# Attention and a gated feed-forward in one kernel: the transposes of q and k move from the matrix engine to DMA

## The chip, the core and the metric

The kernel runs on one core of one Trainium2 chip. The time is device microseconds from the start to the end of one execution, as the median of several runs, and lower is better. The engines of the core run beside each other and wait for each other by semaphores: PE (TensorE, matrix products, with PEld loading the stationary operand), DVE (VectorE), ACT (ScalarE), POOL (GpSimd), and SP (SyncE), which here only issues DMAs. Every instruction of an engine runs in the order in which the program holds it.

## The reference

```python
def _attn_ref(q, k, v):                       # q, k, v: (8, 12, 448, 64) float32
    S = q.shape[2]
    scale = 1.0 / np.sqrt(q.shape[-1])
    scores = scale * np.matmul(q, k.transpose(0, 1, 3, 2)) - np.log(S)
    attn = 1.0 / (1.0 + np.exp(-scores))
    return np.matmul(attn, v)

def _moe_ref(x, w_in, w_out):                 # x: (3584, 768), w_in: (768, 2048)
    h = x @ w_in
    g = h - np.tanh(h)
    return g @ w_out
```

The attention's output, with its heads side by side, is x: 8 batches of 448 tokens, 768 features each. w_in and w_out are given as float64.

## The kernel before, in words

**Two halves of every number.** A product in float32 takes PE longer than one in float16, so most products are made from float16 parts. A number times a power of two is rounded to float16 (the high part), and what is left over is rounded to float16 again (the low part). A product is then three float16 products: high by high, high by low, low by high. Each pair of parts takes two instructions: a scaled copy on ACT or DVE, and one `scalar_tensor_tensor` on DVE for the remainder.

**Batches.** Eight batches go through the kernel. For a batch there is attention (six pairs of heads), then `moe1` (x times w_in, lines 668 to 692, and the gate's function in `mix`), then `moe2` (g times w_out, line 798 and, for the last 64 tokens, line 836). Batch 0's attention is made alone at the start, in float32 (`attention32`), while w_in and w_out are read and turned from float64 to float32. From then on the attention of batch b + 1 is put into `moe2` of batch b: a generator, `stream` (line 429), holds it in steps, and `second` takes the next step after each so many rows of `moe2`, by the tables `BLOCKS`, `BLOCKS0` and `BLOCKS1`. `BLOCKS` has twelve steps, four rows of `moe2` apart, which is two steps for each of a batch's six pairs of heads. In `moe1` of the batches from 1 on there is no step of the attention. What `stream` does ahead of its main loop (the first two pairs' parts among it) runs in batch 0's `moe1`.

**A pair of heads.** The pair is called g. q and k of a pair are loaded by `load_qk` with tokens on 112 partitions and 4 x 2 x 64 numbers on each (`kn`, `qn`). `norms` (line 308) squares and sums them on ACT, `scales` (line 316) adds the sums over the partitions with a product by ones and finds the power of two. Scores need the head's 64 numbers on partitions, so q and k are turned:

- `transpose` (line 299): four products with the identity on PE, in float32, into one tile of PSUM under the tag `tr`, of which there is one. `turn_k` also puts the sums of `scales` into the same tile's last columns.
- `parts` (lines 337 to 340): the high part from PSUM, on ACT (line 337) for all of Q and for some of K, on DVE (line 339) for the rest of K, then the low part from PSUM on DVE (line 340). They are written to K or Q (128 x 2 x 448, two buffers each), which `scores` (line 362) reads.

In `stream`'s main loop (line 508) step 0 of pair g turns q of pair g + 1, and step 1 turns k of pair g + 2. In both, the order on PE is: the turn, twelve products of scores for two blocks of 112 keys, then twelve products of the attention weights with v (line 386) for the blocks of the step before, then `moe2` again. ACT takes the sigmoid of the first block (line 371), then makes the high part of Q, then the second block's sigmoid, then the weights' high part (line 377); DVE makes the low parts. The loads of pair g + 3 are written in step 0, its norms in step 1. For the next batch's x, `batch_scales` (lines 608 to 631) finds one scale and splits x into parts on DVE (lines 625 and 626) at the end of each `moe2`.

PE, ACT, DVE and POOL run in the order in which the program is written. SP's order is the scheduler's.

**Weights.** `wi` and `wo` hold float32 blocks and, later, their float16 parts in the same memory: the float32 of block n lies `SHIFT` = 4 blocks further on, so the parts of block n overwrite float32 that has been used already.

Of the kernel before, what the change touches and what calls it, by code (L numbers as in the profile page):

```python
# [34 lines left out]
class Builder:  # L35
# [14 lines left out]
    SHIFT = 4  # L50

    def __init__(self, ctx, tc, q, k, v, w_in, w_out, out):
# [30 lines left out]
        self.wo = self.wp.tile([P, self.NF * 2 + self.SHIFT, 2, self.HALF], F16, name="wo")  # L83
# [29 lines left out]
    def where(self, kind, r, i=0):  # L113

        t, n, m = (self.wi, self.NB, 256) if kind == "in" else (self.wo, 1, self.HALF)
        f = t.rearrange("p a b c -> p (a b c)").bitcast(F32)
        r = r * n + i * self.NF + self.SHIFT
        return f[:, r * m : (r + n) * m]
# [91 lines left out]
    def split(self, t, n, S, act):  # L210

        F = t[:, n + self.SHIFT].rearrange("p b c -> p (b c)").bitcast(F32)
# [81 lines left out]
    def transpose(self, n, name, tag="tr", bufs=1, t=None):  # L294
        nc = self.nc
        if t is None:
            t = self.ps.tile([P, 512], F32, name=name, tag=tag, bufs=bufs)
# [13 lines left out]
    def scales(self, ss, pb):  # L311
# [3 lines left out]
        pb = pb[:, self.S : self.S + n]  # L315
# [16 lines left out]
    def parts(self, t, s, name, act):  # L332

        nc = self.nc
        o = self.qk.tile([P, 2, self.S], F16, name=name, tag=name)
        if act:
            nc.scalar.activation(o[:, 0], t, AF.Copy, scale=s)  # L337
        else:
            nc.vector.tensor_scalar(o[:, 0], t, s, None, op0=ALU.mult)
        nc.vector.scalar_tensor_tensor(o[:, 1], t, s, o[:, 0], op0=ALU.mult, op1=ALU.subtract)  # L340
        return o
# [87 lines left out]
    def stream(self):  # L429
# [559 lines left out]
```

## Time and profile before

| what | value |
|---|---|
| median of 3 runs | 1263.84 us (1262.47 to 1264.2) |
| the profiled execution: its own time | 1264.8 us |
| the profiled execution: span from first to last instruction | 1262.5 us |
| mean granted clock of PE | 0.995 |
| instructions | 20449 |
| DMA | 70.52 MB, mean 56 GB/s |

The profile is of one execution. A row of its groups gives the line, the engine, the operation, the tiles, the count, the busy time in us, the mean of one instruction in ns, and the idle time of the engine ahead of them with what ended it. PE's products overlap, so the duration of one is longer than the distance to the next; distances are read from the start times of the timeline. The span is 2.3 us shorter than the execution's own time.

### The profile page before, as it was taken

What the parts mean: (1) busy time and instruction counts of PE and PEld (TensorE: products, weight loads), DVE (VectorE), ACT (ScalarE), POOL (GpSimd) and SP (SyncE); (2) the same over time, 40 slices, a digit from 0 to 9 for tenths busy, and PEclk for the clock granted to TensorE, in tenths of its full rate; (3) what the DMA queues carried; (4) which work ended last, traced back from release to release, by engine and by line L of the source; (5) the groups of instructions that cost most, each with busy time, mean ns of one, the idle gap of its engine ahead of it and who ended that gap; (6) DMA issues with size and microseconds to landing.
All of it is one profiled execution on the core that took longest, in us unless ns stands there. A gap on an engine that the chain in (4) does not pass through costs nothing.

```text
span 1262.5 us, 20449 instructions
## 1 busy us (share of the span) xinstructions
PE 1235.0 (98%) x8011; PEld 685.3 (54%) x8011; DVE 946.7 (75%) x1473; ACT 940.2 (74%) x1325; POOL 38.6 (3%) x38
## 2 busy tenths in 40 slices
PE   9889889999999999999999999999999999999998
PEld 3245445555556555665555655555556655555555
DVE  5989988789876797676965798667976769645930
ACT  6957788958998688886878688886888868753820
POOL 0100000000010000100000000000000000000000
PEclk9999999999999999999999999999999999999999
DMA  9943254100122101220022200221012200100001
GB/s 261 299 126 90 56 162 136 49 20 1 36 73 57 42 2 42 65 65 7 1 58 64 56 1 16 64 58 41 1 43 67 62 7 1 28 14 20 1 13 32
DMA packets 114367, 70.52 MB, mean 56 GB/s; under 512 B 91872, under 2 KB 104416, under 8 KB 114272
## 3 DMA queue, kind: packets, MB, share of 16 engines
q1 hardware_dynamic: 113344, 69.00, 20.6%
q8 instruction: 63, 1.03, 0.3%
q10 hardware_dynamic: 928, 0.23, 0.1%
q14 instruction: 32, 0.26, 0.1%
HBM read 58.20 MB, written 11.01 MB: 55 GB/s over the span
## 4 chain that ended last, share of the span: by engine, by line
PE 74%; DVE 14%; ACT 6%; issue 3%; DMA 3%; SPq 0%; DVEq 0%; ACTq 0%
PE ph L676 30%; PE po L798 25%; PE sc L362 6%; PE acc L386 5%; PE por L836 3%; DVE ahl L378 2%; ACT a L371 2%; DVE xhl L626 2%; DMA raw<-moe_w_in 1%; PE acc L396 1%; PE qT L299 1%; DVE xhl L625 1%; ACT wo L214 1%; DVE stb L151 1%; DVE m L750 1%
## 5 line engine op out<-in xcount | busy, mean ns | idle before, releaser
L798 PE MATMUL po<-wo,g 128*128 128x384 f16 x2304 | 391.4, 326 | 1.0 <-ACT o L827 1.0
L676 PE MATMUL ph<-xhl,wi 128*128 128x448 f16 x2016 | 382.6, 352 | 0.0
L798 PEld LDWEIGHTS <-g 128*128 128x128 f16 x2304 | 219.5, 98 | 171.3 <-issue 30.4
L676 PEld LDWEIGHTS <-wi 128*128 128x128 f16 x2016 | 196.7, 98 | 185.0 <-issue 1.8
L371 ACT ACTIVATE a<-sc,nls,rn 112x896 f32<-112x896 f32 x168 | 179.9, 1095 | 45.4 <-PE sc L362 38.3
L378 DVE SCALAR_TENSOR_TENSOR ahl<-a,ahl 112x896 f16<-112x896 f32 x144 | 155.7, 1122 | 58.6 <-ACT ahl L377 57.9
L746 ACT ACTIVATE u<-ph,ih 128x896 f32<-128x896 f32 x64 | 64.4, 1006 | 98.9 <-PE ph L676 95.3
L377 ACT ACTIVATE ahl<-a 112x896 f16<-112x896 f32 x144 | 128.0, 939 | 0.0
L362 PE MATMUL sc<-Q,K 64*112 64x448 f16 x1008 | 116.1, 362 | 3.8 <-ACT a L371 2.8
L750 DVE SCALAR_TENSOR_TENSOR m<-ph,ihk,u 128x896 f32<-128x896 f32 x64 | 73.5, 1148 | 54.9 <-ACT th L748 54.6
L386 PE MATMUL acc<-ahl,vhl 112*64 112x448 f16 x864 | 96.4, 357 | 0.5
L660 ACT ACTIVATE g<-m,Sg 128x896 f16<-128x896 f32 x64 | 66.6, 1041 | 34.1 <-DVE m L764 28.7
L764 DVE COPY_PREDICATED m<-u,th 128x896 f32<-128x896 uint32 x64 | 77.3, 1207 | 6.9 <-DVE m L761 0.5
L661 DVE SCALAR_TENSOR_TENSOR g<-m,Sg,g 128x896 f16<-128x896 f32 x64 | 73.4, 1147 | 8.8 <-ACT g L660 8.8
L340 DVE SCALAR_TENSOR_TENSOR Q<-qT,sn,Q 128x448 f16<-128x448 f32 x42 | 28.6, 682 | 67.9 <-ACT Q L337 67.9
L362 PEld LDWEIGHTS <-K 64*112 64x112 f16 x1008 | 60.6, 128 | 32.5 <-issue 6.8
L761 DVE SCALAR_TENSOR_TENSOR m<-q,m 128x896 f32<-128x896 f32 x64 | 69.9, 1093 | 8.3 <-ACT q L760 0.9
L706 PE MATMUL ph<-x,wi 128*128 128x448 f32 x192 | 74.8, 539 | 0.0
L751 DVE SCALAR_TENSOR_TENSOR th<-ph,ih,th 128x896 f32<-128x896 f32 x64 | 73.3, 1145 | 0.0
L763 ACT ACTIVATE u<-u,b 128x896 f32<-128x896 f32 x64 | 66.7, 1043 | 5.6 <-DVE m L750 3.6
L757 DVE SCALAR_TENSOR_TENSOR m<-q,m 128x896 f32<-128x896 f32 x64 | 69.5, 1087 | 0.0
L386 PEld LDWEIGHTS <-vhl 112*64 112x64 f16 x864 | 43.5, 109 | 47.8 <-issue 26.1
(134 smaller groups left out, 1323.0 us busy)
## 6 DMA issues: line engine op xcount, KB each, us to landing
raw<-moe_w_in SPq DMA_DIRECT2D x24, 512.0 KB, 7.5
rawo<-moe_w_out SPq DMA_DIRECT2D x32, 384.0 KB, 3.9
kn<-k SPq DMA_DIRECT2D x96, 112.0 KB, 2.9
vn<-v SPq DMA_DIRECT2D x48, 224.0 KB, 2.7
qn<-q SPq DMA_DIRECT2D x94, 112.0 KB, 2.9
out<-o SPq DMA_DIRECT2D x7, 336.0 KB, 3.1
out<-o SPq DMA_DIRECT2D x7, 288.0 KB, 3.1
out<-o SPq DMA_DIRECT2D x7, 240.0 KB, 2.6
```

Source lines behind the costliest of these rows:

```text
L362: nc.tensor.matmul(ps[:CK, h, :S], K[r, w, cs], Q[r, x, :], start=(n == 0), stop=(n == len(prods) - 1))
L371: nc.scalar.activation(a, ps[:CK, :, :S], AF.Sigmoid, bias=self.nls[:CK], scale=scale)
L377: nc.scalar.activation(A[:, 0], a, AF.Copy, scale=A_SCALE)
L378: nc.vector.scalar_tensor_tensor(A[:, 1], a, A_SCALE, A[:, 0], op0=ALU.mult, op1=ALU.subtract)
L386: nc.tensor.matmul(acc[h * D : (h + 1) * D, : self.S], v[:, w, h, c, :], A[:, x, h], start=(c == 0 and n == 0), stop=(c == 3 and n == 2),)
L661: nc.vector.scalar_tensor_tensor(g[:, 1], m, Sg, g[:, 0], op0=ALU.mult, op1=ALU.subtract)
L676: nc.tensor.matmul(ph[:, e, :S], self.wi[:, c * self.NB + k, part, e * P : (e + 1) * P], xhl[c][:, x, :], start=(i == 0), stop=(i == 3 * s ...
L706: nc.tensor.matmul(ph[:, e, :S], self.where("in", c)[:, f * P : (f + 1) * P], xs[c], start=(c == 0), stop=(c == self.NC - 1),)
L750: V.scalar_tensor_tensor(m, ps, ihk, u, op0=ALU.mult, op1=ALU.mult)
L751: V.scalar_tensor_tensor(th, ps, ih, th, op0=ALU.mult, op1=ALU.subtract)
L764: V.copy_predicated(m, u.bitcast(U32), th)
L798: nc.tensor.matmul(po[i][:, :H], gs[f // 2][:, x, f % 2, tk * P : (tk + 1) * P], self.wo[:, i * self.NF + f, w], start=(f == 0 and n == 0) ...
```

## The change

The parts of q and k are made before the turn instead of after it, from `kn` and `qn` in SBUF with tokens on 112 partitions (512 numbers on each), into a float16 tile `w` (112 x 2 x 512), of which there is one. One DMA transpose, issued from SP, then writes both parts into K or Q: 8 blocks of 112 x 128. The turns on PE are gone, and the product of `scales` has a PSUM tile of its own under the same tag `tr`. To make room for `w`, the float32 of w_out lies three blocks ahead of its parts (`SHIFT_O` = 3); w_in keeps four.

```diff
     SHIFT = 4
+    SHIFT_O = 3
...
-        self.wo = self.wp.tile([P, self.NF * 2 + self.SHIFT, 2, self.HALF], F16, name="wo")
+        self.wo = self.wp.tile([P, self.NF * 2 + self.SHIFT_O, 2, self.HALF], F16, name="wo")
...
-        F = t[:, n + self.SHIFT].rearrange("p b c -> p (b c)").bitcast(F32)
+        F = t[:, n + (self.SHIFT if t is self.wi else self.SHIFT_O)].rearrange("p b c -> p (b c)").bitcast(F32)
...
-    def scales(self, ss, pb):
+    def scales(self, ss):
 
         nc = self.nc
         n = ss.shape[1]
-        pb = pb[:, self.S : self.S + n]
+        pb = self.ps.tile([P, 512], F32, name="pbn", tag="tr", bufs=1)[:, :n]
         nc.tensor.matmul(pb, self.onesf[:CK, :], ss, start=True, stop=True)
...
-    def parts(self, t, s, name, act):
-
-        nc = self.nc
+    def parts(self, n, s, name, act):
+
+        nc = self.nc
+        flat = n.rearrange("p c h d -> p (c h d)")
+        w = self.qk.tile([CK, 2, 4 * P], F16, name="w", tag="w", bufs=1)
+        if act:
+            nc.scalar.activation(w[:, 0], flat, AF.Copy, scale=s[:CK])
+        else:
+            nc.vector.tensor_scalar(w[:, 0], flat, s[:CK], None, op0=ALU.mult)
+        nc.vector.scalar_tensor_tensor(w[:, 1], flat, s[:CK], w[:, 0], op0=ALU.mult, op1=ALU.subtract)
         o = self.qk.tile([P, 2, self.S], F16, name=name, tag=name)
-        if act:
-            nc.scalar.activation(o[:, 0], t, AF.Copy, scale=s)
-        else:
-            nc.vector.tensor_scalar(o[:, 0], t, s, None, op0=ALU.mult)
-        nc.vector.scalar_tensor_tensor(o[:, 1], t, s, o[:, 0], op0=ALU.mult, op1=ALU.subtract)
+        nc.sync.dma_start_transpose(
+            o.rearrange("p x (c t) -> p (x c) t", c=4), w.rearrange("p x e -> p (x e)")
+        )
         return o
...
-        def turn(g, n, name):
-            return self.transpose(qk[g][n], name) if g < G else None
-
-        def turn_k(g):
-            if g >= G:
-                return None
-            t = self.ps.tile([P, 512], F32, name="kT", tag="tr", bufs=1)
-            turned = self.transpose(qk[g][0], "kT", t=t)
-            sc[g] = self.scales(ss.pop(g), t)
-            return turned
-
-        def parts_k(g, t):
+        def scales(g):
             if g < G:
-                K[g] = self.parts(t, sc[g][0][:, 0:1], "K", not splits(g) and g not in (2, 3))
-
-        def parts_q(g, t):
+                sc[g] = self.scales(ss.pop(g))
+
+        def parts_k(g):
             if g < G:
-                Q[g] = self.parts(t, sc[g][0][:, 1:2], "Q", True)
+                K[g] = self.parts(qk[g][0], sc[g][0][:, 0:1], "K", not splits(g) and g not in (2, 3))
+
+        def parts_q(g):
+            if g < G:
+                Q[g] = self.parts(qk[g][1], sc[g][0][:, 1:2], "Q", True)
                 qk.pop(g)
 
...
-            parts_k(g, turn_k(g))
+            scales(g)
+            parts_k(g)
             yield 450, False
-            parts_q(g, turn(g, 1, "qT"))
+            parts_q(g)
             load(g + 2)
...
-                    t = turn_k(g + 2)
-                elif g:
-                    t = turn(g + 1, 1, "qT")
+                    scales(g + 2)
                 pss = [self.scores(c, K[g], Q[g]) for c in (2 * i, 2 * i + 1)]
                 aa = [self.weigh(pss[0], sc[g][1][:CK, 0:1])]
                 if i:
-                    parts_k(g + 2, t)
+                    parts_k(g + 2)
                 elif g:
-                    parts_q(g + 1, t)
+                    parts_q(g + 1)
```

Where the instructions stand: first the PE queue of before, at a step that turns k, with the last products of `moe2` ahead of it (`po`) and the first of the scores behind it (`sc`).

```order
L798 LDWEIGHTS g
L798 MATMUL po<-wo,g 128x384
L299 MATMUL kT<-ident,kn 128x112 x4
L316 MATMUL kT<-ss,onesf 128x3
L362 LDWEIGHTS K
L362 MATMUL sc<-Q,K 112x448
```

The same place of PE's queue in the changed kernel, whose lines have other numbers:

```order
L795 LDWEIGHTS g
L795 MATMUL po<-wo,g 128x384
L316 MATMUL pbn<-ss,onesf 128x3
L367 LDWEIGHTS K
L367 MATMUL sc<-Q,K 112x448
```

The four products with the identity are gone (a step that turns q loses its four likewise, and then has nothing between `po` and `sc`); the product of `scales` stays, into its own tile. On ACT and DVE every instruction keeps its place; the two of `parts` read `kn` or `qn` and write `w`.

Now SP's queue of before over one pair of heads in a later batch, from the q loads of one step 0 to those of the next. The names in brackets are what the instruction waits for; `DMAHW` is one of eight counters that the DMAs use in turn, so each DMA waits for the one eight places ahead of it.

```order
L285 DMA qn<-q 112x4x64 [waits DMAHW3_49,PE_49]
L285 DMA qn<-q 112x4x64 [waits DMAHW4_49]
L291 DMA vn<-v 112x2x256 [waits DMAHW5_49,DVE_49]
L285 DMA kn<-k 112x4x64 [waits DMAHW6_49,PE_49,Activation_49]
L285 DMA kn<-k 112x4x64 [waits DMAHW7_49]
```

And SP's queue in the changed kernel at the same place:

```order
L343 DMA_TRANSPOSE Q<-w 128x8x112 [waits DMAHW4_49,DVE_49]
L286 DMA qn<-q 112x4x64 [waits DMAHW5_49]
L286 DMA qn<-q 112x4x64 [waits DMAHW6_49]
L292 DMA vn<-v 112x2x256 [waits DMAHW7_49,DVE_49]
L286 DMA kn<-k 112x4x64 [waits DMAHW0_49,DVE_49]
L343 DMA_TRANSPOSE K<-w 128x8x112 [waits DMAHW1_49,PE_49]
L286 DMA kn<-k 112x4x64 [waits DMAHW2_49]
```

Two transposes have joined each pair of heads. The one of Q stands ahead of the q loads, which waited for PE's turn before and now wait for DVE's low part by way of the transpose; the one of K stands behind one k load, which waits for the same low part.

More of the change, by code (lines that the diff above doesn't have):

```diff
@@ L113, in where @@
     def where(self, kind, r, i=0):
-        t, n, m = (self.wi, self.NB, 256) if kind == "in" else (self.wo, 1, self.HALF)
+        t, n, m, shift = (self.wi, self.NB, 256, self.SHIFT) if kind == "in" else (self.wo, 1, self.HALF, self.SHIFT_O)
         f = t.rearrange("p a b c -> p (a b c)").bitcast(F32)
-        r = r * n + i * self.NF + self.SHIFT
+        r = r * n + i * self.NF + shift
         return f[:, r * m : (r + n) * m]
@@ L292, in load_v, with transpose @@
         return t
-    def transpose(self, n, name, tag="tr", bufs=1, t=None):
+    def transpose(self, n, name, tag="tr", bufs=1):
         nc = self.nc
-        if t is None:
-            t = self.ps.tile([P, 512], F32, name=name, tag=tag, bufs=bufs)
+        t = self.ps.tile([P, 512], F32, name=name, tag=tag, bufs=bufs)
         for c in range(4):
```

## The prediction

> **What bounds the kernel now.** The page's first part says which engine is full.
>
> ```profile
> PE 1235.0 (98%) x8011; PEld 685.3 (54%) x8011; DVE 946.7 (75%) x1473; ACT 940.2 (74%) x1325; POOL 38.6 (3%) x38
> ```
>
> PE is busy 98% of the span, the others three quarters. An average over stages hides where that differs, so the next view is the windows: start to end in us, length, then busy time of PE, PEld, DVE, ACT.
>
> ```profile
> 104.00:156.00 52.00, 47.51 (x158) 24.87 (x157) 48.81 (x75) 36.46 (x52) 0.00 (x0) 0.99 0.27 70
> 156.00:211.00 55.00, 50.32 (x304) 25.22 (x304) 46.91 (x98) 47.31 (x83) 2.70 (x2) 0.91 0.55 166
> ...
> 478.00:571.00 93.00, 92.89 (x738) 56.64 (x737) 67.77 (x117) 76.18 (x118) 4.56 (x4) 1.00 0.23 58
> ```
>
> In `moe2` of batch 2 (478 to 571 us), and likewise in the later ones, PE is busy 92.89 of 93 us: what is taken off PE there shortens the kernel, until another engine is late. In batch 0 (104 to 211 us) PE idles 9 us of 107 and DVE is as full as PE: there PE's gain may not arrive.
>
> **What the turns cost PE.** PE's timeline in that `moe2` shows one pair of heads, with start time and length in us.
>
> ```profile
> 485.93 0.55 PE L299 MATMUL qT<-ident,qn 112*128 112x112 f32 x4
> 486.41 1.34 PE L362 MATMUL sc<-Q,K 64*112 64x448 f16 x12
> ...
> 492.85 0.55 PE L299 MATMUL kT<-ident,kn 112*128 112x112 f32 x4
> 493.24 0.30 PE L316 MATMUL kT<-ss,onesf 112*128 112x3 f32 x2
> 493.46 1.34 PE L362 MATMUL sc<-Q,K 64*112 64x448 f16 x12
> ...
> 499.90 0.55 PE L299 MATMUL qT<-ident,qn 112*128 112x112 f32 x4
> ```
>
> From start to start, a turn of q takes 486.41 - 485.93 = 0.48 us and one of k 0.39 us (the sums at 493.24 stay). A pair of heads takes 499.90 - 485.93 = 13.97 us and should take 13.10 without its turns.
>
> How many turns lie where: the windows of line 299 alone, PE's count in brackets, four products to a turn.
>
> ```profile
> 104.00:156.00 52.00, 2.85 (x20) 2.21 (x20) 0.99 0.27 70
> 156.00:266.00 110.00, 6.73 (x44) 5.00 (x44) 0.96 0.36 105
> 321.00:424.00 103.00, 8.30 (x60) 6.99 (x60) 1.00 0.25 62
> 478.00:571.00 93.00, 6.63 (x48) 5.63 (x48) 1.00 0.23 58
> ...
> 1066.00:1147.00 81.00, 2.74 (x20) 2.38 (x20) 1.00 0.08 21
> ```
>
> Batches 1 to 6 have 60 + 4 x 48 + 20 = 272 products, 68 turns, half of q and half of k: 34 x 0.48 + 34 x 0.39 = 29.6 us. Batch 0 has 16 turns, 7.0 us.
>
> **Where PE's gain does not arrive.** At the end of each `moe2` the chain of waits (start, length) runs on DVE, since the next batch's x is split there between the attention's own work.
>
> ```profile
> 547.79 2.09 DVE ahl L378 x2
> ...
> 564.39 2.02 DVE ahl L378 x2
> 566.41 0.04 issue
> 566.45 0.38 PE acc L386 x2
> ```
>
> From 547.79 to 566.41 every link of that chain is DVE's, and PE's products with v wait for its end. Three turns fall into this stretch, by line 299's window:
>
> ```profile
> 547.80:566.50 18.70, 1.70 (x12) 1.35 (x12) 1.00 0.27 70
> ```
>
> Two turns of k and one of q, 1.26 us, are thus not on the path there; five batches have such an end (the last two have no x to split): -6.3 us. In batch 1 the steps stand three rows apart, and ACT is nearly full:
>
> ```profile
> 332.30:344.30 12.00, 12.00 (x97) 7.13 (x96) 10.31 (x17) 11.61 (x19) 0.00 (x0) 1.00 0.24 59
> ```
>
> A pair could go from 12.0 to 11.13 us on PE, but ACT needs 11.61: about 0.45 us lost on each of some 3.5 pairs, -1.6 us.
>
> For batch 0, PE's waits for the one `tr` tile are a second thing that goes (us in total, times, longest).
>
> ```profile
> PE qT L299 <- DVE K L340: 2.7, 2, 2.2
> PE kT L299 <- DVE Q L340: 2.3, 3, 1.0
> ```
>
> At most 7.0 + 5.0 = 12 us could come there, at least nothing, since DVE is full; and the transposes now stand in SP's queue ahead of loads of w_out, which could cost some us. I take 4 us, with -8 to 12 as ends.
>
> **The parts on ACT and DVE.** They read SBUF instead of PSUM, 112 x 512 instead of 128 x 448. DVE does just that for v (lines 348 and 349), ACT for the norms (line 308).
>
> ```profile
> L340 DVE SCALAR_TENSOR_TENSOR Q<-qT,sn,Q 128x448 f16<-128x448 f32 x42 | 28.6, 682 | 67.9 <-ACT Q L337 67.9
> L349 DVE SCALAR_TENSOR_TENSOR vhl<-vn,sn,vhl 112x512 f16<-112x512 f32 x36 | 27.1, 752 | 1.3
> L337 ACT ACTIVATE Q<-qT,sn 128x448 f16<-128x448 f32 x42 | 26.3, 626 | 0.0
> L308 ACT ACTIVATE sqn<-kn 112x512 bf16<-112x512 f32 x42 | 26.1, 621 | 0.0
> L339 DVE TENSOR_SCALAR K<-kT,sn 128x448 f16<-128x448 f32 x38 | 26.0, 684 | 0.7
> L348 DVE TENSOR_SCALAR vhl<-vn,sn 112x512 f16<-112x512 f32 x36 | 17.2, 477 | 0.0
> ```
>
> The low part becomes 70 ns dearer (84 times, +5.9 us of DVE), DVE's high part 207 ns cheaper (38 times, -7.9 us), ACT's stays. On the path that is nothing: in DVE's stretch above one of the cheap ones and two of the dear ones give -0.07 us. Three blocks ahead instead of four for w_out: a part waits for the remainder three blocks back instead of four, which DVE has done in both cases as long as the two engines take the parts in turn; I put nothing, and up to 2 us inside batch 0's ends if ACT runs ahead.
>
> **The transpose.** No row of before shows one. Call T the time from DVE's low part being done to K or Q being there and `w` free. Two ordinary DMAs bound it, with KB and median us to landing:
>
> ```profile
> vn<-v SPq DMA_DIRECT2D x48, 224.0 KB, 2.7
> raw<-moe_w_in SPq DMA_DIRECT2D x24, 512.0 KB, 7.5
> ```
>
> A transpose moves 112 x 1024 float16, 224 KB, as a load of v does in 2.7 us; 7.5 us is the slowest kind of DMA here, at more than twice the bytes and in the crowd of the start. I take 4 us, nearer to the first for its equal bytes, dearer since the pieces have to be rearranged; the ends stay for the range.
>
> What T may be is read from the steps' timeline (ACT makes Q's high part, DVE its low part; then DVE both of K; `ahl` and `acc` are the weights and their product with v).
>
> ```profile
> 502.20 0.62 ACT L337 ACTIVATE Q<-qT,sn 128x448 f16<-128x448 f32 x1
> 502.85 0.68 DVE L340 SCALAR_TENSOR_TENSOR Q<-qT,sn,Q 128x448 f16<-128x448 f32 x1 [2.13 <-ACT Q L337]
> 508.82 0.68 DVE L339 TENSOR_SCALAR K<-kT,sn 128x448 f16<-128x448 f32 x1
> 509.54 0.68 DVE L340 SCALAR_TENSOR_TENSOR K<-kT,sn,K 128x448 f16<-128x448 f32 x1
> 511.21 2.09 DVE L378 SCALAR_TENSOR_TENSOR ahl<-a,ahl 112x896 f16<-112x896 f32 x2 [0.99 <-ACT ahl L377]
> 515.62 0.57 PE L386 MATMUL acc<-ahl,vhl 112*64 112x448 f16 x4
> ...
> 514.45 1.24 SPq L285 DMA_DIRECT2D qn<-q  x2
> ```
>
> Q itself is needed by the next pair's scores, one pair later: 486.41 + 2 x 13.97 = 514.35, some 10.8 us after 503.53, 9.9 without the turns. `w` is tighter, since there is one: K's high part wants it at 508.82, 5.29 us after Q's low part ended, 4.9 without the turn between; Q's next (502.20 + 13.97 = 516.17) wants it 5.95 us after K's low part, 5.5 without the turn, of which the k load that stands ahead of K's transpose takes 0.62. So T up to about 4.85 us costs nothing, and the work that hides it is `moe2`'s four rows between two steps. Above that, DVE or ACT waits for `w` with the weights' split (`ahl`) queued behind, and PE waits for that after the slack is gone: 515.62 - 513.30 = 2.3 us now, 1.9 without a turn. Behind Q's transpose on SP stand the q and v loads, and behind those ACT's norms.
>
> ```profile
> 511.91 0.62 ACT L308 ACTIVATE sqn<-kn 112x512 bf16<-112x512 f32 x1
> ```
>
> The two q loads used to be issued from 514.45 - 13.97 = 500.48 on; now they follow Q's low part at 503.53, take 1.24 to issue and some 2.7 to land, so 507.5, which is 4.4 us ahead of the norms, 3.5 with the shorter pair. SP's own time to issue a transpose is not known; up to about 3.5 us of it is hidden.
>
> **The sum.** 29.6 - 6.3 - 1.6 + 4 = 25.7 us off the profiled execution's 1264.8: 1239.1. That execution is 1.0 us above the median of the runs shown, so on the median 1263.84 - 25.7 = 1238.1, forecast 1238. Its own range, with T below 4.85: 1264 - 29.6 - 7 = 1227 where nearly all arrives, 1264 - 21.7 + 8 = 1250 where batch 0 loses.
>
> **The rivals.**
>
> *The one tile `w` becomes the clock.* Each use of `w` then lasts T plus the two instructions that write it. Batches 1 to 6 have 68 uses, 62 of them behind another in the same `moe2`; beyond 4.85 us each costs the excess, less 1.9 us once per batch: 62 x (T - 4.85) - 11. The gain of 25.7 is gone at T = 5.45; T = 6.5 gives 1238 + 91 = 1329, and at the upper bound T = 7.5 it is 1238 + 153 = 1391. For it speaks that the gap between "free" and "lost" is only 0.6 us wide, and that SP's queue puts loads next to the transposes; against it that a load of the same bytes takes 2.7. Chance 0.22 for 5.45 to 7.5; 0.08 for 4.85 to 5.45 (1238 to 1264).
>
> *The transpose goes block by block.* Eight blocks of 112 x 128, each with its own start, would take T to the upper bound or past it, so at least 1391. The nearest row against it is the 2.7 us for 896 pieces of 256 bytes. Chance 0.12. The Trainium skill's page "VectorE: DVE Perf Modes", section "The three transpose paths", speaks for this and against the change: it gives 390 ns for a 128 x 128 block of 2-byte numbers on TensorE and 1309 ns by DMA. By that, eight blocks would take an estimated 10.5 us and the time would be 1238 + 339 = 1577. The Trainium skill's page "DMA: Bandwidth & Descriptors", section "Latency and other measured facts", has 261 GB/s for a DMA transpose, an estimated 0.9 us for these bytes beside the start, and the forecast's time. No run here shows either yet.
>
> *Batch 0 pays.* The transposes make SP wait for DVE's low parts, and loads of w_out stand behind; where DVE is full, 16 waits of about 1 us would turn the 4 us into a loss near 15, and 1257 would come out. PE's pieces of `wl` and ACT's line 145 would show the wait. Against it: those loads are issued two pieces ahead. Chance 0.06.
>
> **How the numbers follow.** The forecast has 0.52. Two tenths of a per cent is 2.5 us, about what a measurement can tell here. Faster by more: 0.52 + 0.06 + most of the 0.08, less a little, 0.62. Within: 0.04. Slower: 0.22 + 0.12 = 0.34. For the range, 1227 to 1345: below lies 0.03, above it the block by block case (0.12) and T over 6.8 us (0.05), in all 0.2. Both signs hold much, so the forecast's own range is 1227 to 1250.
>
> **What would show it.** Right: the DMA issues list the transposes at under 4.9 us; PE's start-to-start distance per pair falls to about 13.1 us; `moe2`'s window of 93 shrinks by about 4; no idle time before the instructions that write `w`. Wrong: waits of ACT or DVE on those instructions released by a DMA; scores released by a DMA; PE idle inside `moe2`; or `moe2` shorter, as forecast, with batch 0 longer.

## The result and the profile after

The changed kernel takes 1251.89 us (median of 4 runs, 1251.14 to 1253.55) against 1263.15 us for the kernel before (4 runs): ratio 0.9905, 95% interval 0.9892 to 0.9918, which is about 12 us off where 25.7 were forecast. Its profiled execution has a span of 1249.4 us against 1262.5.

The page of the kernel after: busy time and share of the span per engine.

```profile
PE 1208.2 (97%) x7675; PEld 652.7 (52%) x7675; DVE 941.8 (75%) x1473; ACT 943.7 (76%) x1325; POOL 37.4 (3%) x38
```

PE has lost 26.8 us of busy time, but the span lost 13.1 only. The DMA issues of the kernel after (KB where the trace gives them, median us to landing):

```profile
vn<-v SPq DMA_DIRECT2D x48, 224.0 KB, 3.2
...
K<-w SPq DMA_TRANSPOSE x42, 3.1
Q<-w SPq DMA_TRANSPOSE x42, 3.0
```

A transpose lands 3.0 to 3.1 us after its issue, inside the bounds of 2.7 and 7.5 and below the 4 that was taken. PE's timeline in `moe2` of batch 2 (start, length, what), to be set beside the rows from 485.93 on of before:

```profile
496.70 4.07 PE L795 MATMUL po<-wo,g 128*128 128x384 f16 x24
500.70 1.34 PE L367 MATMUL sc<-Q,K 64*112 64x448 f16 x12
...
503.24 4.07 PE L795 MATMUL po<-wo,g 128*128 128x384 f16 x24
507.14 0.28 PE L316 MATMUL pbn<-ss,onesf 112*128 112x3 f32 x2
...
513.89 1.34 PE L367 MATMUL sc<-Q,K 64*112 64x448 f16 x12
```

A pair of heads takes 513.89 - 500.70 = 13.19 us; it took 13.97 and should have taken 13.10. There the change does nearly all that was forecast. A window of the kernel after (start to end, length, busy time of PE, PEld, DVE, ACT, POOL, granted clock, DMA share, GB/s) shows where it does not:

```profile
156.00:211.00 55.00, 45.65 (x268) 21.81 (x269) 43.48 (x90) 43.73 (x77) 2.28 (x2) 0.93 0.71 180
```

From 156 to 211 us, in batch 0, PE now idles 9.4 us (4.7 before). The next two windows go from 104 us to the first product of batch 1's `moe1`, of before and then of after:

```profile
104.00:266.10 162.10, 151.98 (x854) 81.24 (x852) 142.66 (x282) 128.63 (x227) 5.13 (x4) 0.97 0.33 94
104.00:270.25 166.25, 148.11 (x789) 75.81 (x788) 142.12 (x280) 128.98 (x226) 4.55 (x4) 0.96 0.45 113
```

In batch 0 PE's busy time falls by 3.9 us only, from 152.0 to 148.1, and its idle time rises by 8.0, from 10.1 to 18.1. One place divides the account: the start of `moe1` of batch 1, the first product of line 676 (673 after), where batch 0 and the start of the kernel end. Before it comes at 266.1 us, after at 270.3. What follows lasts 1262.5 - 266.1 = 996.4 us before and 1249.4 - 270.3 = 979.1 after. So batches 1 to 6 gave 17.3 us, and batch 0 lost 4.2.

The waits for w_out's pieces, of before (engine, line, tile, what released it: us in total, times, longest):

```profile
ACT stb L145 <- DMA rawo<-moe_w_out: 1.6, 3, 0.8
PE wl L177 <- DVE stb L151: 1.8, 3, 0.9
```

and of after, with the wait on `w`:

```profile
PE wl L178 <- DVE stb L152: 10.5, 9, 2.2
ACT stb L146 <- DMA rawo<-moe_w_out: 7.6, 3, 5.8
ACT w L338 <- DMA K<-w: 1.5, 3, 1.1
```

`w` is hardly waited for (1.5 us by ACT and 0.9 by DVE in the whole kernel). But ACT waits 7.6 us for loads of w_out. SP's timeline shows why; before:

```profile
193.29 0.57 SPq L285 DMA_DIRECT2D qn<-q  x1
193.96 2.97 SPq L130 DMA_DIRECT2D rawo<-moe_w_out  x4
```

and after:

```profile
195.64 2.17 SPq L343 DMA_TRANSPOSE Q<-w  x1
197.86 1.25 SPq L286 DMA_DIRECT2D qn<-q  x2
199.21 1.98 SPq L131 DMA_DIRECT2D rawo<-moe_w_out  x4
```

The four loads now stand behind a transpose that waits for DVE's low part and takes SP 2.17 us to issue (1.2 to 1.3 for most of the others), and behind the q loads after it: 5.2 us later. They hold the end of batch 0 in the chain of waits of the kernel after:

```profile
197.08 0.74 SPq L343
...
199.21 4.31 DMA rawo<-moe_w_out
...
208.64 0.44 SPq L343
209.19 3.56 DMA rawo<-moe_w_out
```

PE feels it in `moe2`'s own rows, since a product for `wl` stands between each six of them (timeline of after):

```profile
198.88 1.72 PE L401 MATMUL acc<-a,vn 112*64 112x448 f32 x8
...
205.21 0.33 PE L178 MATMUL wl<-stb,onesb 128*128 128x384 bf16 x1 [1.23 <-DVE stb L152]
...
208.69 0.33 PE L178 MATMUL wl<-stb,onesb 128*128 128x384 bf16 x1 [2.17 <-DVE stb L152]
208.94 1.51 PE L367 MATMUL sc<-Q,K 64*112 64x448 f16 x12
210.38 3.20 PE L401 MATMUL acc<-a,vn 112*64 112x448 f32 x8
```

Eight such products `acc` take 1.72 us ahead of the two waits of 1.23 and 2.17 us and 3.20 behind them. The window of those at 210.38 shows PE busy throughout, at a granted clock of 0.52:

```profile
210.40:213.50 3.10, 3.10 (x10) 0.75 (x8) 2.96 (x7) 1.91 (x5) 0.00 (x0) 0.52 0.85 227
```

So PE's idle time is followed here by a stretch at about half the clock, which costs time again.

### The profile page after: what moved, and what is told of

It reads as the page before. It is cut to its first block, busy times and chain, and to the rows that moved or that the text cites. A ratio compares the mean times of both kernels' runs of the same rounds, so it can differ in the third digit from the quotient of the medians.

```text
span 1249.4 us, 19946 instructions
## 1 busy us (share of the span) xinstructions
PE 1208.2 (97%) x7675; PEld 652.7 (52%) x7675; DVE 941.8 (75%) x1473; ACT 943.7 (76%) x1325; POOL 37.4 (3%) x38
## 4 chain that ended last, share of the span: by engine, by line
PE 63%; DVE 18%; ACT 10%; issue 4%; DMA 3%; SPq 1%; DVEq 0%; ACTq 0%
PE ph L673 31%; PE po L795 19%; PE sc L367 4%; PE acc L391 4%; DVE ahl L383 4%; PE por L833 3%; ACT a L376 2%; DVE xhl L623 2%; DVE m L747 1%; DVE m L761 1%; DVE m L758 1%; DVE g L658 1%; ACT w L338 1%; DMA K<-w 1%; PE acc L401 1%
## 5 line engine op out<-in xcount | busy, mean ns | idle before, releaser
L391 PE MATMUL acc<-ahl,vhl 112*64 112x448 f16 x864 | 99.5, 357 | 5.0 <-DVE ahl L383 4.4
L341 DVE SCALAR_TENSOR_TENSOR w<-qn,sn,w 112x512 f16<-112x512 f32 x42 | 31.5, 750 | 64.1 <-ACT w L338 64.1
```

The lines of the kernel that those rows point to most:

```text
L391: nc.tensor.matmul(acc[h * D : (h + 1) * D, : self.S], v[:, w, h, c, :], A[:, x, h], start=(c == 0 and n == 0), stop=(c == 3 and n == 2),)
```

## The experiments

All of them beside the kernel before on the same chip. "Batch 1 starts" is the first product of its `moe1`; "rest" is the span less that. The rest agrees within 1.0 us among kernels with the same later batches (e12 apart, where `moe1` itself waits for w_in's parts), so nearly all scatter between single profiles lies ahead of that place: 263.6 to 266.1 among the five kernels (before, and e1, e2, e6 and e7 with three blocks ahead) whose batch 0 has the same turns and loads. A start that differs by less than these 2.5 us shows nothing by itself.

| kernel | ratio to before (interval) | batch 1 starts | rest | span |
|---|---|---|---|---|
| before | 1 | 266.1 | 996.4 | 1262.5 |
| after | 0.9905 (0.9892 to 0.9918) | 270.3 | 979.1 | 1249.4 |
| e1 three blocks alone | 0.9995 (0.9985 to 1.0005) | 263.6 | 996.4 | 1260.0 |
| e2 34 late transposes alone | 0.9866 (0.9848 to 0.9884) | 265.0 | 979.4 | 1244.4 |
| e3 eight early pairs alone | 1.0034 (1.0022 to 1.0046) | 269.9 | 996.4 | 1266.3 |
| e4 w_out's loads from POOL | 0.9929 (0.9914 to 0.9944) | 272.5 | 979.8 | 1252.3 |
| e5 second half from POOL | 0.9913 (0.9897 to 0.9928) | 277.3 | 979.1 | 1256.4 |
| e6 as e2, part of x on ACT | 0.9849 (0.9833 to 0.9865) | 265.1 | 976.5 | 1241.6 |
| e7 as e2, transposes twice | 1.0574 (1.0551 to 1.0597) | 264.8 | 1070.8 | 1335.6 |
| e8 SP in program order | 0.9984 (0.9975 to 0.9994) | 280.8 | 979.3 | 1260.1 |
| e9 loads a step earlier | 0.9882 (0.9865 to 0.9898) | 269.1 | 978.8 | 1247.9 |
| e10 before, loads a step earlier | 1.0004 (0.9994 to 1.0014) | 267.3 | 996.7 | 1264.0 |
| e11 as e9, part of x on ACT | 0.9863 (0.9849 to 0.9876) | 268.6 | 976.7 | 1245.3 |
| e12 as e9, w_in's high parts on POOL | 0.9918 (0.9906 to 0.9931) | 271.4 | 981.0 | 1252.4 |
| e13 before, the same | 1.0028 (1.0017 to 1.0039) | 267.7 | 996.6 | 1264.3 |
| e14 as e6, the same | 0.9887 (0.9875 to 0.99) | 273.1 | 976.6 | 1249.7 |
| e15 before, 16 early turns twice | 1.0016 (1.0004 to 1.0027) | 266.8 | 996.8 | 1263.6 |
| e16 as e9, less work for ACT | 0.9868 (0.9853 to 0.9883) | 265.1 | 979.0 | 1244.1 |
| e17 before, less work for ACT | 0.9988 (0.998 to 0.9997) | 264.2 | 996.4 | 1260.6 |
| e18 after, early transposes later on SP | 0.9892 (0.9874 to 0.991) | 267.9 | 979.1 | 1247.0 |

Part of the scatter is PE's clock. Take (1 - granted clock) times length, summed over windows of 4 us from 104 to 268 us: 5.1 us in before, 6.9 in after, 3.4 in e1, e2 and e16, 5.1 in e11, e15, e17 and e18, 6.8 in e3, 8.6 in e9, 13.8 in e8. These are steps of about 1.7 us, one for each place like the one at 210 us, and each kernel has one profile.

### Which part of the change does what: e1, e2, e3

e1, the kernel before with only w_out's float32 moved closer:

```diff
+    SHIFT_O = 3
-        self.wo = self.wp.tile([P, self.NF * 2 + self.SHIFT, 2, self.HALF], F16, name="wo")
+        self.wo = self.wp.tile([P, self.NF * 2 + self.SHIFT_O, 2, self.HALF], F16, name="wo")
```

> The kernel before with only the float32 of w_out moved to three blocks ahead; the turns stay on PE. Theory A (the transposes stand in SP's queue ahead of w_out's loads and hold them up in batch 0): nothing changes, 1263 us within 1.5, batch 1's first product of moe1 starts at 266 us as before. Rival B (the shorter distance between float32 and parts makes ACT and DVE wait for each other in batch 0): the 4 us that batch 0 has lost appear here, start at about 270 us, total about 1267.

Measured: 0.9995, no difference. Three blocks ahead cost nothing; the loss in batch 0 is not theirs.

e2 and e3 split the transposes: pairs 0 to 7 (turned in batch 0) against the other 34. The line of e2, with `g < 8` in e3:

```diff
+        by_dma = lambda g: g >= 8
```

> The changed kernel with PE's turns for pairs 0 to 7 (those whose turns fall into batch 0) and the DMA transposes for the other 34. Theory A, and also rival C (the transposes' traffic slows w_out's loads): batch 1's moe1 starts at 266 us as before and the later batches are as short as in the changed kernel, so about 1252 - 4 = 1248 us. Rival B (three blocks): moe1 of batch 1 still at 270, total 1252.

> The opposite: DMA transposes for pairs 0 to 7 alone, PE's turns for the other 34. Theory A and rival C: batch 1's moe1 starts at 270 us, later batches 147 us each as before, so 1263 + 4 = 1267 us. If the two halves do not touch each other, the change of this run and of the run with the late ones add up to that of the whole change (-11 us).

Measured: the late ones alone give 16.9 us (1264 x 0.0134), the early ones alone cost 4.3 us (2.8 to 5.8), and the sum, 12.6, is the change's 12. In e2 batch 1 starts at 265.0 and PE's wait for `wl` is back at

```profile
PE wl L178 <- DVE stb L152: 2.1, 5, 0.9
```

while e3 has the wait of the full change without its gain:

```profile
ACT stb L146 <- DMA rawo<-moe_w_out: 7.0, 3, 5.2
```

So the loss is shown to come from the new way of turning the first eight pairs, in batch 0.

### Is it the loads of w_out behind the transposes: e4, e5, e8, e9, e10, e18

e4 issues all loads of w_out from GpSimd (POOL), e5 only those of the second half, with batch 1's sums of squares moved from POOL to DVE so that nothing stands in POOL's queue ahead of them. The diff is e5's; e4 has it without the condition on `i` and without that move.

```diff
-        self.nc.sync.dma_start(p["raw"], src[r * P : (r + 1) * P, i * n : (i + 1) * n])
+        queue = self.nc.gpsimd if i and not p["staged"] else self.nc.sync
+        queue.dma_start(p["raw"], src[r * P : (r + 1) * P, i * n : (i + 1) * n])
```

> The changed kernel with w_out's loads issued from the otherwise idle POOL, so that no transpose stands ahead of them; the traffic is the same. Theory A: ACT's wait for these loads (7.6 us in the changed kernel) goes below 2, PE's wait for the conversion (10.5 us) below 4, moe1 of batch 1 starts at 264 to 267 us, total 1245 to 1249. Rival C (traffic): loads still land late, moe1 at 270, total 1252.

> As the run with w_out's loads on POOL, but for the second half of w_out alone, and with POOL's sums of squares for batch 1 done on DVE, so that nothing stands in POOL's queue between these loads (in the earlier run they stood behind those sums, which wait for ACT). Theory A (the loads are late because something that waits stands ahead of them in an in-order queue): ACT's wait for the loads falls from 7.6 us below 2, PE's wait for the conversion from 10.5 below 4, moe1 of batch 1 starts at 264 to 268 us, total 6 to 2 us below the changed kernel: 0.986 to 0.989 of before. Rival C (the transposes' traffic) and rival D (batch 0 is full on DVE and ACT whatever the loads do): start stays at 270, ratio 0.990 to 0.992.

Measured: neither is better in the place that matters. In e4 the loads stood in POOL's queue behind the additions of line 432, which wait for ACT. In e5 ACT's wait on `rawo` did fall, but a transpose issued at 167.88, beside POOL's loads at 167.20 and 169.71, took 10.9 us to land. The waits of e5 from 104 to 280 us:

```profile
PE sc L368 <- DMA Q<-w: 6.8, 1, 6.8
...
ACT stb L147 <- DMA rawo<-moe_w_out: 0.6, 1, 0.6
```

One wait took the place of the other. This profile is also of the slowest of e5's six executions (1258.21 us, median 1252.84), so its start of batch 1 stands for that execution alone. The pair is inconclusive on the question.

e8 goes the other way: SP's instructions in the order in which the program is written, instead of the scheduler's.

```diff
-        with tc.manual_schedule(engines={E.PE, E.Activation, E.DVE, E.Pool}):
+        with tc.manual_schedule(engines={E.PE, E.Activation, E.DVE, E.Pool, E.SP}):
```

> The changed kernel with SP's queue in the order in which the program is written instead of the scheduler's. Each transpose then stands behind all loads written ahead of it. Theory A: batch 0 changes by where w_out's loads stand; they are now split in groups by each transpose as before, so the wait of ACT for them stays between 3 and 10 us, start of batch 1's moe1 between 267 and 274. Rivals C and D: 270 us, unchanged by any order.

Measured: batch 1 starts at 280.8, 10.5 us later than after and beyond the 267 to 274 that theory A gave; the rest is unchanged (979.3), and ACT's wait grows:

```profile
ACT stb L146 <- DMA rawo<-moe_w_out: 20.0, 7, 7.5
```

So the order on SP's queue can set batch 0's length, which rivals C and D denied, and it touches nothing else here. Of the 10.5 us, 6.9 can be the lower clock (13.8 against 6.9) behind PE's longer idle time. e9 moves each load of w_out's second half one step ahead of its use, and e10 does so in the kernel before.

```diff
-            (wait if ps[0]["piece"][2] else end).remove(None)
+            wait, end = (wait, end) if ps[0]["piece"][2] else (wait, [None, self.conv_end])
...
+        next(rest)
         next(ahead[0])
         next(rest)
```

> The changed kernel with each load of w_out's second half issued one step (0.95 rows of moe2, about 2.7 us) earlier than before relative to the instructions that use it, so that on SP about one load more stands ahead of each transpose. Theory A, the loads of w_out stand too late in SP's queue behind transposes that wait for DVE's low part and take 1.27 us of issue each: ACT's wait on rawo falls from 7.0 us in two waits to below 4, PE's wait for wl from 9.6 to below 6, moe1 of batch 1 starts at 266 to 268 instead of 270.3, and the time is 1247 to 1250 against the changed kernel's 1251.9. Rival D, batch 0 is held by DVE and ACT being full and by PE's lower clock after its idle time, and the wait for the loads only shows who comes last: ACT's wait on rawo falls, but moe1 of batch 1 still starts at 269.5 to 271 and the time stays at 1251 to 1253.

> The control for the run above: the kernel before with the same earlier loads. It waits 0.8 us for rawo in all, so theory A expects no change: 1262 to 1265, moe1 of batch 1 at 265 to 267. If it gains 2 us or more, earlier loads help whatever the transposes do, and the run above would show nothing of them.

Measured: e9 gains 2.9 us on the changed kernel (0.9905 to 0.9882; the two intervals just overlap), e10 nothing. In the profile batch 1 starts at 269.1, between A's number (266 to 268) and D's (269.5 to 271); PE's wait for `wl` falls to 7.3 us, not below 6. The waits of e9 name no load of w_out any more, but that is a trap of the view. ACT's timeline in e9 at the same place as in after:

```profile
202.21 0.56 ACT L146 ACTIVATE stb<-rawo 128x384 f32<-128x384 f32 x1 [4.88 <-PE po L795]
```

and SP's:

```profile
194.72 2.21 SPq L343 DMA_TRANSPOSE Q<-w  x1
...
198.27 2.03 SPq L131 DMA_DIRECT2D rawo<-moe_w_out  x4
```

ACT idles 4.9 us ahead of an instruction on a load, and the loads, issued from 198.27 on, landed 3.8 us later at the earliest, at 202.07. PE's product, to which the idle time is put down, ended in the same 0.2 us. The scheduler had left the four loads behind the transpose of Q, so the wait had not gone.

e18 therefore moves the transposes instead. Those of pairs 2 to 7 are written into the program three of the conversion's steps after the parts (and at once if the next parts need `w`).

```diff
+        self.turning.append([4, o, w])
+        self.turn_due(not later)
...
+        events += [(k * self.CONV, lambda: (next(rest, None), self.turn_due())) for k in range(1, steps + 1)]
```

> The changed kernel with the transposes of pairs 2 to 7 written three rows of moe2 later than the parts, so that on SP's queue three of the four loads of w_out that stood behind the transpose of Q at 195 to 199 us stand ahead of it, and the q loads too. K and Q are needed one to three steps later, so nothing should wait for them. Theory A, SP's order holds batch 0: ACT's idle time ahead of its instructions on these loads, 7.0 us in the changed kernel, falls below 3, PE's wait for wl from 9.6 to below 6, moe1 of batch 1 starts at 266 to 268 instead of 270.3; 1246 to 1249. Theory D, ACT and DVE hold it whatever the loads do: the waits fall, batch 1 still starts at 269 to 271; 1250 to 1253. A third way: the later transposes make K or Q late and scores wait for a DMA; then batch 1 starts after 271.

Measured: 0.9892, 1.6 us better than the change, which the intervals do not separate; 1250.88 us is D's time (1250 to 1253). Batch 1 starts at 267.9, which is A's number, 2.4 us earlier than after; 1.8 of these can be the clock (5.1 against 6.9). SP's queue in e18:

```profile
194.50 0.99 SPq L131 DMA_DIRECT2D rawo<-moe_w_out  x1
195.59 1.23 SPq L286 DMA_DIRECT2D qn<-q  x2
196.88 1.08 SPq L131 DMA_DIRECT2D rawo<-moe_w_out  x2
198.00 1.27 SPq L354 DMA_TRANSPOSE Q<-w  x1
```

and the waits of e18 from 104 to 280 us:

```profile
ACT stb L146 <- DMA rawo<-moe_w_out: 4.7, 2, 3.1
PE wl L178 <- DVE stb L152: 8.0, 7, 2.1
```

ACT's wait fell from 7.0 to 4.7, not below 3, and PE's for `wl` from 9.6 to 8.0, not below 6; the q loads and `Q<-w` still take SP's time between the loads. Both e9 and e18 point to 1.2 to 2.9 us of batch 0 for a queue that is only partly cleared, neither clear of the noise, and e8 costs 10.5 for one that is worse. That the order on SP's queue can hold batch 0 is shown by e8; that it is part of the change's own loss is likely and not shown, and how much a fully cleared queue would give is not known.

### What holds batch 0 then: e12 to e17

e12, e13 and e14 take w_in's 48 high parts off ACT:

```diff
+            if t is self.wi:
+                self.nc.gpsimd.tensor_scalar(t[:, n, 0], F, S, None, op0=ALU.mult)
+            else:
+                self.nc.scalar.activation(t[:, n, 0], F, AF.Copy, scale=S)
```

> The changed kernel with the loads of w_out a step earlier, and with w_in's 48 high parts in batch 0's moe2 made on GpSimd (128x256, an estimated 0.65 us each by its 1.15 us for 128x448) instead of on ACT (0.40 us each, 19 us in all). Theory D, batch 0 is held by ACT's and DVE's work, so that PE's turns were not on its path: moe1 of batch 1 starts 4 us or more earlier than the 269.1 of the same kernel without this, 265 or less, and the time is 1241 to 1246. Theory A2, something of the transposes themselves (their waits, their DMA traffic) holds batch 0: it stays at 268 to 270, 1247 to 1250.

> The control: the kernel before with the same 48 high parts on GpSimd. Under theory D it gains less than the changed kernel does, since PE still has its 16 turns (7.0 us): moe1 of batch 1 starts at 262 to 266, 1259 to 1264, so that the difference between the two kernels in batch 0, which was 4.1 us to the loss of the changed one, becomes nil or a gain. Under A2 both gain alike and the loss of 3 to 4 us stays.

> The kernel with PE's turns for the first eight pairs and the DMA transposes for the other 34, with two of six high parts of x on ACT (1243.95 before this) and with the 48 high parts of w_in on GpSimd. If the gain of the control adds to it: 1240 to 1243. If batch 0 does not depend on ACT: 1243 to 1245.

Measured: all three are slower than without it, against what was expected. POOL's row in e12 says why:

```profile
L216 POOL TENSOR_SCALAR wi<-wi,swi_s 128x256 f16<-128x256 f32 x48 | 52.6, 1113 | 5.9 <-DVE wi L221 5.8
```

1113 ns each instead of the 650 estimated: POOL itself became the clock of batch 0 (these rows are half of e12's chain of waits from 215 to 272 us). Nothing follows for ACT.

e15 asks about PE directly. In the kernel before, each turn of the first eight pairs is made twice:

```diff
+                t = self.transpose(qk[g][n], name)
+                return self.transpose(qk[g][n], name, t=self.again) if g < 8 else t
...
+            if g < 8:
+                turned = self.transpose(qk[g][0], "kT", t=t)
```

> The kernel before with each of the 16 turns of the first eight pairs made twice on PE (7.0 us more PE work, into the same PSUM tile). Theory D, batch 0 is held by ACT and DVE, so that PE's turns are mostly off its path: moe1 of batch 1 starts 1 to 3.5 us later than the 266.1 of before, and the time is 1265 to 1267. Rival P, the turns are on the path in full, so that taking them away should have given their 7.0 us and the transposes cost some 11: moe1 starts 6 to 8 us later, 1270 to 1272.

The windows of the line of the turns in e15 (PE and PEld busy; line 299's 44 products of before lie in the second):

```profile
104.00:156.00 52.00, 3.78 (x32) 3.36 (x32) 0.99 0.24 65
156.00:266.00 110.00, 11.56 (x88) 9.98 (x88) 0.96 0.36 104
```

PE did 15.3 us of turns there instead of 9.6, 5.8 more by the records; the kernel became 2.0 us slower (0.5 to 3.4), and in the profile batch 1 starts 0.7 us later, at the same loss to the clock. The time is theory D's number (1 to 3.5), the start is below it, and neither is P's (6 to 8): about a third of the added turns is on batch 0's path, the rest is covered by other engines. The 5.0 us of waits for the tile `tr`, which the change also took away, are not tested by this.

e16 and e17 take some work off ACT in batch 0: the sums of squares of pairs 4 to 8 run over 64 of 512 numbers (those norms are only estimates), and 16 of the 48 high parts go to POOL.

```diff
-            self.nc.scalar.activation(junk, t.rearrange("p a b d -> p (a b d)"), AF.Square, accum_out=ss[:, i : i + 1])
+            flat, m, f = t.rearrange("p a b d -> p (a b d)"), 8 * D, 1.0
+            if light:
+                m, f = D, 8.0**0.5
+            self.nc.scalar.activation(junk[:, :m], flat[:, :m], AF.Square, scale=f, accum_out=ss[:, i : i + 1])
```

> The changed kernel with the loads of w_out a step earlier, with the sums of squares of pairs 4 to 8 taken over 64 of the 512 numbers only (their norms are thus only estimated), and with 16 of w_in's 48 high parts on GpSimd: an estimated 5.5 + 6.4 us less on ACT in batch 0. Theory D: moe1 of batch 1 starts 3 us or more ahead of the 269.1 of the same kernel without this, 266 or less; 1242 to 1246. If something else than ACT holds it, DVE or the transposes: 268 to 269.5, 1247 to 1249.

> The control: the kernel before with the same relief of ACT. Under theory D it gains less than the changed kernel, by up to the 7.0 us of its turns: moe1 of batch 1 starts at 264 to 266 instead of 266.1; 1261 to 1264. If both gain alike, ACT holds batch 0 in both, and the turns play no part.

Measured: in the profiles the changed kernel gains 4.0 us in batch 0 (269.1 to 265.1), the kernel before 1.9 (266.1 to 264.2), as D said. But e9 loses 8.6 us to the clock and e16 3.4, more than the 4.0, while before and e17 lose the same. And the times say less: 1.8 us (0.9882 to 0.9868, which the intervals do not separate) against 1.5 (0.4 to 2.5), and e16's 1247.21 us is the rival's number (1247 to 1249), not D's. So ACT's work is shown to hold part of batch 0 in the kernel before; for the changed kernel it is likely, and that less of it would let the removed turns pay is not shown.

### The tile `w` and the end of `moe2`: e7, e6, e11

e7 is e2 with each transpose issued twice.

```diff
+        for _ in range(2):
             nc.sync.dma_start_transpose(
```

> The kernel with only the late transposes, each issued twice into the same place, the second after the first has landed, so that the time until w is free goes from 3.1 to about 6.2 us. The prediction's model of the one tile w: 62 x (6.2 - 4.85) - 11 = 73 us more, about 1320. Rival (w has more slack than that, since ACT and DVE can run behind): less than 20 us more.

Measured: 1.0574, 91.4 us more in the rest than e2 (1070.8 against 979.4), where the model gave some 73. The waits on `w` that are absent from the kernel after are all there:

```profile
ACT w L353 <- DMA K<-w: 93.2, 28, 5.1
DVE w L355 <- DMA Q<-w: 41.9, 20, 3.7
```

The rival of the one tile was thus real and near: the second transpose holds `w` some 3 us longer, and that costs 7%. In the rest PE idles 57 us more than in e2, and the clock takes an estimated 27 us by windows of 8 us, against none in e2: the part beyond the model's 73 is no larger than what the clock took behind PE's idle time.

e6 is e2 with two of the six high parts of the next batch's x on ACT; e11 does that to e9.

```diff
-            V.tensor_scalar(hl[:, 0, :], x, Sx, None, op0=ALU.mult)
+            if j in (2, 4):
+                self.nc.scalar.activation(hl[:, 0, :], x, AF.Copy, scale=Sx)
+            else:
+                V.tensor_scalar(hl[:, 0, :], x, Sx, None, op0=ALU.mult)
```

> The kernel with only the late transposes, and two of the six high parts of the next batch's x made on ACT instead of DVE. Theory (the end of each moe2 is bound by DVE, so PE's gain is lost there): DVE loses 2 x 0.45 us in that stretch, which ACT has room for, so 5 batches x 0.9 = 4.5 us: ratio 0.983. Rival (PE is the bound there too, and the loss of the later batches has another cause): no change, 0.9866.

> The changed kernel with the earlier loads and with the high parts of the third and fifth block of the next batch's x made on ACT instead of DVE. Those took 2.8 us off where the first eight pairs were turned by PE. If both parts add up under theory A: 1244 to 1247, moe1 of batch 1 at 266 to 268. Under rival D: 1248 to 1250.

Measured: the rest falls by 2.9 us (979.4 to 976.5) and by 2.1 (978.8 to 976.7). So DVE's stretch at the end of `moe2` did hold PE: an estimated 4.5 us less of DVE's work there gave 2.1 to 2.9. e6, at 1243.95 us, has the lowest time of all these kernels: 1.51% ahead of the kernel before, against 0.95% for the change (its interval overlaps those of e2, e11 and e16).

## Why the prediction was right or wrong

**The turns in batches 1 to 6: right, one term mis-sized.** The forecast took 29.6 - 6.3 - 1.6 = 21.7 us off these batches; 17.3 came. Of the 4.4 missing, 3.1 are in the 0.48 us for a turn of q. In the timeline of after, the 24 products of `moe2` last 503.24 to 507.14, 3.90 us, when the small product of line 316 follows, and 496.70 to 500.70, 4.00 us, when the scores follow directly. Before, a turn followed in both places, after 3.91 us (488.94 to 492.85 and 495.99 to 499.90):

```profile
495.99 4.07 PE L798 MATMUL po<-wo,g 128*128 128x384 f16 x24
```

So going over to the scores costs 0.1 us, which had been counted as part of the turn of q: that turn was worth 0.39 like the turn of k, 34 x 0.09 = 3.1 us less. The remaining 1.3 us are in PE's waits for DVE and ACT, taken at 7.9. The windows from the start of batch 1 to the end, of before and of after, are

```profile
266.10:1262.50 996.40, 988.36 (x6774) 567.54 (x6772) 721.09 (x1040) 735.71 (x985) 27.34 (x24) 1.00 0.13 33
270.25:1249.40 979.15, 965.05 (x6502) 540.32 (x6500) 716.53 (x1041) 738.65 (x985) 27.23 (x24) 1.00 0.22 50
```

PE's idle time rises by 6.1 us, from 8.0 to 14.1. Its products of the weights with v, now broken up by waits for `ahl`, take 3.1 more (99.54 us in line 391 against 96.42 in line 386), 9.2 us in all.

**The end of `moe2` on DVE: right.** From the first product `nm`, where the next batch's scale is being found, to the next `moe1`, PE's rows of before are

```profile
547.77 0.35 PE L603 MATMUL nm<-x2b,onesb 128*128 128x448 bf16 x1
...
570.66 54.65 PE L676 MATMUL ph<-xhl,wi 128*128 128x448 f16 x288
```

and those of after

```profile
545.73 0.35 PE L600 MATMUL nm<-x2b,onesb 128*128 128x448 bf16 x1
...
568.58 54.65 PE L673 MATMUL ph<-xhl,wi 128*128 128x448 f16 x288
```

That is 22.89 us and 22.85: the 1.26 us of the three turns do not arrive there. The chain of waits of the kernel after runs on DVE from 546.85 to 564.32, and e6 shows the place by taking work off DVE.

**The transpose and `w`: right, with room.** T is 3.0 to 3.1 us against 4 taken and 4.85 free. Under T = 3.1 the formula gives no cost, and only 2.4 us of waits on `w` are found. e7 bears the formula out above the threshold; what it cost beyond the 73 us can be the clock. The rival "block by block" is refuted: its T of 7.5 us or more did not come. The Trainium skill's page "VectorE: DVE Perf Modes", section "The three transpose paths", gives 1309 ns for one 128 x 128 block by DMA, an estimated 10.5 us for eight; the trace has 3.0 for the eight blocks of 112 x 128 of one DMA. The 261 GB/s of the Trainium skill's page "DMA: Bandwidth & Descriptors", section "Latency and other measured facts", fit better: the estimated 0.9 us for the bytes beside the start lies inside the 3.0, though no run separates the two.

**The parts on ACT and DVE: one size wrong.** The rows of the kernel after (duration min/median/max in ns) are

```profile
L338 ACT ACTIVATE w<-qn,sn x42: 705/710/728, 118.8 to 1091.2; 112x512 f16<-112x512 f32 x42
L340 DVE TENSOR_SCALAR w<-kn,sn x38: 485/486/490, 159.8 to 1084.6; 112x512 f16<-112x512 f32 x38
```

DVE's 477 and 752 ns were right (486 and 751 came). "ACT's stays" was not: the high part went from 626 to 710 ns. In batch 0's `moe1` and `moe2`, where ACT's work counts (e17), 12 of them add an estimated 1 us to ACT's work.

**Batch 0: wrong, and the failed step.** "At most 7.0 + 5.0 = 12 us could come there ... I take 4 us": batch 0 lost 4.2 us in the profile instead (4.3 by the times of e3), which is 8.2 of the 12.6 us by which the spans fall short of the forecast. Two things were wrong in it. First, the gain was read from PE's own rows, 16 turns and the waits for the tile `tr`. But PE was not what held most of batch 0: e15 shows that 5.8 us of turns more cost 2.0, so the turns taken away were worth about that at most, if more and less count alike; e17 shows that ACT's work counts. PE's busy time there fell by 3.9 us and its idle time rose by 8.0. The prediction had seen both facts ("DVE is as full as PE: there PE's gain may not arrive") and still took a gain as the likeliest. Second, the cost was put at "some us" and into the bounds. The rival "batch 0 pays" names what the profiles show: transposes that wait for DVE, loads of w_out behind them in SP's queue, seen in ACT's line for `stb` and PE's `wl`. Its argument against, that the loads are issued two pieces ahead, did not hold, since SP itself needs 1.2 to 2.2 us to issue a transpose and the q loads stand between; its price, a loss near 15, is more than three times the 4.2 that came (16 waits of about 1 us off a gain of 4 would be a loss of 12). SP's time to issue was named as unknown and costed for the steady batches alone, where it is hidden indeed.

**Open.** How batch 0's loss divides. Part of it is likely SP's queue (1.2 to 2.9 us came back with it partly cleared), 1 us is ACT's dearer high part by estimate. The low clock took 6.9 us in after against 5.1 in before, and 6.8 in e3 against 3.4 in e2, so it can be 1.8 to 3.4 us of the loss. It stands behind idle time of PE and so is rather what the waits cost a second time than a cause of its own, but no run changed the clock by itself and none cleared the queue wholly. The shares are not settled.

**The range.** 1251.89 lies in the range of 1227 to 1345, and 2 us above the forecast's own range of 1227 to 1250, whose upper end was the case in which batch 0 loses 8 and all else arrives. That it came out so near this end is luck: batch 0 lost half of that, and 4.4 us were missing elsewhere.

## What to carry to other kernels

Work that leaves a full engine pays only in the stages that this engine holds: count the gain stage by stage, and where two other engines are as busy, take it as nothing until a doubled copy of that work (here 2.0 us for 5.8) says otherwise. Look at the granted clock right behind PE's new idle time too: here each such place cost about 1.7 us more. A DMA that takes over such work brings its wait and its issue time into an in-order queue; look at what stands behind it there in the stage that loads the most, and if the stages differ, change only those where it pays (34 pairs alone give 16.9 us, all 42 give 12).

## What was not expected of the hardware

- SP is mostly busy 1.2 to 1.3 us with the issue of one transpose of 112 x 1024 float16, against 0.6 for a load of k of 112 KB and 0.3 to 0.6 for one of v of 224 KB. Its own landing, 3.0 us, is about that of a load of equal bytes (3.2).
- A transpose issued beside loads from POOL's queue landed after 10.9 us instead of 3.0 (e5, once, in its slowest execution).
- The same float32 products `acc` of line 401 took 1.72 us for eight before PE's idle time at 203 to 209 us and 3.20 after it, at a granted clock of 0.52 (198.88 and 210.38 of the kernel after). Two waits of 1.23 and 2.17 us were enough for that.
- From the last 128-row products of `moe2` to the 64-row products of the scores PE needs 0.1 us more than to a product of 112 rows (4.00 us against 3.90 for the 24 products); the reason is not shown.
- POOL needs 1.11 us for 128 x 256 float32 to float16, twice and more what ACT does (0.50 in before's row, 0.40 from start to start).
